# A gated recurrence with a highway layer on one core: units of eight blocks joined in pairs on freely named PSUM banks, and outputs stored by 1 MB transfers

## The chip, the cores and the metric

The kernel runs on one core of one Trainium2 chip. The metric is the device time of one execution in microseconds (us). A core has five engines with their own instruction streams: TensorE (PE, its weight loads shown apart as PEld), VectorE (DVE), ScalarE (ACT), GpSimd (POOL) and SyncE (SP, which here only issues transfers). PSUM is the accumulator memory, eight banks of 2 KB in each of 128 partitions; SBUF is the working memory.

## The reference

Four sequences of 6336 steps and 256 channels go through a gated recurrence, and each token of the result through a highway layer. Inputs and output are float32.

```python
def _attn_ref(x, f_logit, lower_bound):
    sig = 1.0 / (1.0 + np.exp(-f_logit))
    f = lower_bound[None, None, :] + (1.0 - lower_bound[None, None, :]) * sig
    i = 1.0 - f
    for t in range(S):
        h = f[:, t] * h + i[:, t] * x[:, t]
        y[:, t] = h
    return y

def _moe_ref(x, w_h, w_t, b_t):          # x is y as (25344, 256)
    H = np.maximum(x @ w_h, 0.0)
    T = 1.0 / (1.0 + np.exp(-(x @ w_t + b_t)))
    return T * H + (1.0 - T) * x
```

## The kernel before

With cc = 1 - lower_bound, the kernel takes u = sigmoid(-f_logit), so that i = cc u and f = 1 - cc u (ncc is -cc). The scan runs on y/cc, and cc is multiplied into the weights, into a diagonal matrix `diag` and into d.

The 25344 tokens are cut into 198 blocks of 128, and these into 28 units (`parts`, L42) of 2, 2, 4, then 23 times 8, then 4 and 2 blocks. A token of the stream lies in a partition with its neighbours: in a unit of eight blocks partition p holds eight tokens in a row, so that a load is 1 MB of 8 KB rows. Each unit passes through these steps, most of them once for each half h of the channels:

- l, x: one transfer each, issued on SP (L232 to L242).
- u: sigmoid on ACT, all of the unit at once (L247).
- b: products u x, in bf16 with two tokens packed side by side, on POOL, or on DVE where the token has a v (L250 to L257). Their tile is bv.
- i: PE transposes u into uT (PSUM, L259 to L263). f: 1 - cc uT, on ACT or DVE (L265 to L274).
- p: PE transposes the packed pairs of bv as float32 words into bT (PSUM, L276 to L283).
- s: the scan y = f y + bT on DVE, 1024 tokens in one instruction, chained to the unit before (L295 to L301).
- z, g: matmuls of y with the two weights (L303 to L320; L113 is the same matmul without a new load of weights). t: sigmoid of z, on ACT (L322 to L324). d: max(ncc y, g) on DVE (L326 to L329). e: d = d t, in two pieces, on POOL or DVE (L331 to L334).
- o: output matmuls that turn blocks back to token rows, with columns of y and d as weights and `diag` and an identity as data, four blocks in one two-bank PSUM tile op (L339 to L349). A block's columns lie `g` apart, and g is 4 in a unit of eight blocks.
- c: copy of op to an SBUF tile o of 4 KB a partition (L351 to L358). w: its store, 512 KB in 4 KB rows, issued on SP (L360 to L362).

The loops are written out as one string, `order`: each token is a step letter, a unit, a half or piece, and a buffer slot. All steps are pinned, so each engine runs its instructions in the order of the string, and SP issues loads and stores in that order too. Tokens k are idle matmuls that keep PE going. `shared` (L176) makes a POOL instruction follow a DVE one.

PSUM is split into two slots of one bank (a0, a1: uT and bT) and three of two banks (b0 to b2: z, g and op). SBUF has four o tiles of 4 KB. In the middle of the program l uses three buffers and x four.

Of the kernel before, what the change touches and what calls it, by code (L numbers as in the profile page):

```python
# [11 lines left out]
FP32 = mybir.dt.float32  # L12
# [7 lines left out]
def kernel(  # L20
# [10 lines left out]
    nc = tc.nc  # L31
# [10 lines left out]
    parts = [2] * 2 + [4] + [8] * 23 + [4] + [2]  # L42
    units, at = [], 0
    for nb in parts:
        units.append((nb, at, {2: (0, 1), 4: (0, 1, 2), 8: (0, 2, 4)}[nb], {2: (0, 256, 512), 4: (0, 512, 1024), 8: (0, 1024, 2048)}[nb]))
        at += nb * P
# [3 lines left out]
f0.0v:0 x5:5 f0.1v:1 WH p0.0:0 WT p0.1:1 k*4:0 s0.1:0 l6:5 x6:0 i2.0:1 b1.0:0 s0.0 f2.0:1 i1.0:0 z0.1:0 f1.0v:0 g0.1:1  # L50
g0.0:2 d0.1:0 b2.0:1 d0.0 p1.1:1 t0.1:0 i1.1:0 z0.0:0 k*4:1 b2.1 f1.1v:2 s1.1:1 p1.0:0 t0.0 p2.0:1 s1.0 e0.0 s2.0:2
z1.1:0 e0.1 u3:0 i2.1:0 z1.0:1 g1.1:2 b3.0:0 d1.1:1 p2.1:1 f2.1:0 g1.0:2 s2.1 t1.0:0 b3.1v d1.0 i3.0:0 k*4:1 t1.1
f3.0:1 g2.0:0 o0.0:1 i3.1:0 e1.1 e1.0 u4:1 d2.0:0 f3.1:0 p3.0:1 c0.0:0 s3.0:0 b4.1:1 z2.1:2 k*4:0 o1.0:0 b4.0 p3.1:0
s3.1 z2.0:1 w0.0 l7:0 t2.1:0 g2.1:2 c1.0:1 d2.1 i4.0:1 t2.0 k*4:0 e2.0 f4.0:1 e2.1 g3.0:0 w1.0 p4.0:0 u5:0 i4.1:1
z3.0:1 f4.1:0 b5.1:0 o2.0:2 p4.1:1 b5.0 t3.0:0 c2.0:2 w2.0 g3.1:1 x7:1 d3.0:1 s4.0:1 s4.1 u6:1 l8:1 i5.1:0 z3.1:0
p5.1:1 e3.0v f5.1:1 t3.1 z4.1:2 i5.0:0 b6.0:1 d3.1 f5.0:0 e3.1 g4.1:1 g4.0:0 t4.1:1 x8:2 u7:0 p5.0:0 s5.1:2 i6.0:1
d4.1:0 f6.0:1 o3.1*1:2 z4.0:1 s5.0 i7.0:1 d4.0 b6.1 c3.1:0 p6.0:0 s6.0:3 e4.1 z5.1:2 w3.1 b7.0:0 g5.1:0 l9:0 f7.0:0
d5.1:2 i6.1:1 t4.0 g5.0:1 i7.1:0 t5.1:0 f6.1:2 d5.0 o3.0:2 b7.1 p6.1:1 f7.1:1 x9:0 c3.0:1 e4.0v w3.0 e5.1 l10:2 u8:0
z5.0:0 p7.0:0 o4.1:1 s6.1 o4.0:2 c4.1:0 t5.0 i8.1:1 c4.0:2 s7.0:0 g6.0:1 u9:1 w4.1 f8.1:0 w4.0 g6.1:0 p7.1:0 l11:1
b8.1:1 x10:1 d6.0:0 b8.0 z6.0:2 s7.1 t6.0:1 z6.1:1 e5.0 i9.0:1 e6.0 p8.1:0 f9.0:1 o5.1:2 i8.0:1 d6.1 t6.1 f8.0:2  # L60
c5.1:0 g7.1:0 e6.1 w5.1 k*4:1 b9.0:0 p8.0:1 u10:0 s8.1:1 z7.0:1 t7.0:0 d7.1:1 i9.1:0 o6.1:0 s8.0 g7.0:2 c6.1v:1 l12:0
# [24 lines left out]
p22.1:1 t21.0:0 o19.1:2 l25:1 o19.0:1 d21.1:1 w18.0 w18.1 x24:0 p23.1:0 u25:0 s22.1 c19.0:0 b24.0:0 s23.1:2 g22.0:0
d22.0:2 i23.0:1 z22.0:1 x25:2 c19.1:1 z22.1:2 f23.0:0 p23.0:0 i25.0:1 t22.0:2 o20.0:0 g22.1:1 s23.0 w19.0 b24.1 t22.1
e22.0 g21.0:2 i24.0:0 c20.0:2 d22.1 g23.1:0 f25.0:1 w19.1 f24.0:0 i24.1:1 d21.0 d23.1:3 l26:0 e22.1v x26:1 f24.1:2
o20.1:1 g23.0:2 d23.0 p24.0:0 s24.0:1 b25.0:1 i25.1:1 c20.1:0 w20.0 l27:1 b25.1 z23.1:0 u26:1 f25.1:3 z21.1:1 p24.1:1
x27:3 o22.0:2 t23.1:1 b26.0:0 s24.1 e21.0v t21.1 c22.0:1 z23.0:0 p25.0:0 e21.1 o22.1:1 t23.0 z24.1:2 u27:0 i26.0:1  # L90
g24.0:0 s25.0:0 c22.1:2 f26.0:0 b26.1 z24.0:1 d24.0:0 p25.1:1 t24.1:2 i26.1:0 w20.1 e23.0 t24.0 o21.0:2 e23.1 g24.1:0
f26.1:1 c21.0:0 e24.0 o21.1:1 s25.1 p26.0:0 c21.1:3 p26.1:1 d24.1 s26.1:3 z25.1:2 w22.0 t25.1:0 g25.1:0 w22.1 w21.0
d25.1:1 o23.0:1 w21.1 s26.0 o23.1:2 i27.1:1 c23.0:1 z25.0:0 b27.0:0 w23.0 c23.1:0 g26.0:1 g25.0:2 t25.0 e24.1v d26.0:2
d25.0 i27.0:0 e25.1 e25.0v w23.1 f27.0:0 z26.1:0 o24.0:1 f27.1:1 p27.0:0 p27.1:1 z26.0:2 s27.0:2 s27.1 t26.1:1 c24.0:2
o25.0:0 t26.0 g26.1:1 w24.0 o24.1:2 d26.1 z27.0:1 c24.1v:0 c25.0:1 t27.0:0 o25.1:0 c25.1:3 e26.0 g27.0:1 d27.0:0 e26.1
o26.0:2 w25.0 w24.1 z27.1:1 t27.1 e27.0v c26.0:2 w25.1 w26.0 g27.1:0 d27.1 e27.1v o27.0:0 c27.0:1 w27.0
"""

    NU = len(units)
# [3 lines left out]
    st = [dict() for _ in range(NU)]  # L103
# [15 lines left out]
    extra = [0]  # L119

    def busy(t):
        for k in range(extra[0]):
            if k == 0:
                pin(nc.tensor.matmul(t[:, :512], zeros[:, :P], zeros, start=True, stop=True))
            else:
                pin(again(t[:, :512], zeros[:, :P], zeros, True, True))

    def one_bank(slot, dtype, name):
        t = ps.tile([P, NB * P], dtype, tag=f"a{slot}", name=name)
        busy(t.bitcast(FP32))  # L130
        return t

    def two_banks(slot, name):
        t = ps.tile([P, NB * P], FP32, tag=f"b{slot}", name=name)
        busy(t)
        return t
# [13 lines left out]
    for _ in range(8):  # L150
        nc.tensor.matmul(once["idle"][:, :512], zeros[:, :P], zeros, start=True, stop=True)
# [251 lines left out]
```

## Time and profile before

| | |
|---|---|
| median of 3 runs | 212.07 us (211.65 to 212.75) |
| span of the profiled execution, first to last instruction | 209.0 us |
| the profiled execution's own time | not recorded; the median is 3.1 us above its span |
| granted TensorE clock | 0.998 |
| busy: PE, DVE, ACT, POOL | 197.0, 194.8, 191.1, 176.2 us |
| DMA | 78.67 MB, 376 GB/s over the span |

Rows of the profile read so: a line of the kernel, an engine, an operation, the tiles written and read with partitions x elements, the count; behind the first bar the busy time in us and the mean ns of one; behind the second the idle time of the engine just before, and what ended it. A busy PE counts overlapped matmuls once. In a row of the time line the start and the duration come first. A row on a DMA has the issuing queue, the count, the KB of each and the median us from issue to landing.

### The profile page before, as it was taken

What the parts mean: (1) busy time and instruction counts of PE and PEld (TensorE: products, weight loads), DVE (VectorE), ACT (ScalarE), POOL (GpSimd) and SP (SyncE); (2) the same over time, 40 slices, a digit from 0 to 9 for tenths busy, and PEclk for the clock granted to TensorE, in tenths of its full rate; (3) what the DMA queues carried; (4) which work ended last, traced back from release to release, by engine and by line L of the source; (5) the groups of instructions that cost most, each with busy time, mean ns of one, the idle gap of its engine ahead of it and who ended that gap; (6) DMA issues with size and microseconds to landing.
All of it is one profiled execution on the core that took longest, in us unless ns stands there. A gap on an engine that the chain in (4) does not pass through costs nothing.

```text
span 209.0 us, 4656 instructions
## 1 busy us (share of the span) xinstructions
PE 197.0 (94%) x1852; PEld 135.3 (65%) x1852; DVE 194.8 (93%) x159; ACT 191.1 (91%) x185; POOL 176.2 (84%) x101
## 2 busy tenths in 40 slices
PE   7989998999899999899999999999999999999991
PEld 2446575686576577558676667575677776777680
DVE  0789999999999999999999999999999999999971
ACT  4368999999999999999999999999999999997972
POOL 3076998989997887997999899788999999989740
PEclk9999999999999999999999999999999999999999
DMA  6999999999999999999999999999999999655567
GB/s 174 367 419 423 416 417 421 416 423 372 422 408 351 387 427 413 416 417 412 410 420 416 423 418 424 408 425 412 426 421 400 379 405 341 267 204 201 199 278 279
DMA packets 15980, 78.67 MB, mean 376 GB/s; under 512 B 1748, under 2 KB 2264, under 8 KB 10072
## 3 DMA queue, kind: packets, MB, share of 16 engines
q1 hardware_dynamic: 15952, 78.39, 93.6%
q8 instruction: 14, 0.23, 0.5%
q14 instruction: 6, 0.05, 0.1%
q10 hardware_dynamic: 8, 0.00, 0.0%
HBM read 52.43 MB, written 25.95 MB: 375 GB/s over the span
## 4 chain that ended last, share of the span: by engine, by line
PE 50%; DVE 14%; ACT 12%; DMA 9%; issue 8%; POOL 4%; SPq 1%; DVEq 0%; ACTq 0%; POOLq 0%
DVE y L299 10%; PE op L347 7%; PE op L348 7%; PE z L311 7%; PE bT L282 6%; DMA x<-in_x_dram 6%; PE z L113 6%; PE g L311 6%; PE g L113 5%; PE uT L262 5%; ACT f L273 4%; DVE d L328 4%; ACT o L357 4%; POOL bv L255 3%; DMA l<-in_f_logit_dram 3%
## 5 line engine op out<-in xcount | busy, mean ns | idle before, releaser
L255 POOL TENSOR_TENSOR bv<-u,x 128x1024 bf16<-128x1024 f16 (+1 forms) x51 | 103.2, 2046 | 17.2 <-DVE y L299 9.3
L299 DVE TENSOR_TENSOR_SCAN y<-f,y,bT 128x1024 bf16<-128x1024 f16 (+5 forms) x54 | 106.8, 1991 | 1.0 <-PE bT L282 0.3
L334 POOL TENSOR_TENSOR d<-d,t 128x1024 bf16<-128x1024 bf16 (+2 forms) x39 | 73.0, 1888 | 7.8 <-DVE d L334 4.1
L328 DVE SCALAR_TENSOR_TENSOR d<-y,ncc,g 128x1024 bf16<-128x1024 bf16 (+2 forms) x56 | 62.9, 1140 | 1.6 <-PE g L311 1.0
L324 ACT ACTIVATE t<-z,bt 128x1024 bf16<-128x1024 f32 (+2 forms) x56 | 58.4, 1075 | 2.3 <-PE z L311 1.9
L273 ACT ACTIVATE f<-uT,ncc 128x1024 f16<-128x1024 f16 (+2 forms) x51 | 56.4, 1120 | 3.5 <-PE uT L262 3.2
L247 ACT ACTIVATE u<-l 128x2048 f16<-128x2048 f32 (+2 forms) x28 | 49.6, 1774 | 5.1 <-DMA l<-in_f_logit_dram 4.5
L357 ACT COPY o<-op 128x1024 f32<-128x1024 f32 (+1 forms) x48 | 48.9, 1047 | 2.3 <-PE op L348 1.7
L347 PE MATMUL op<-diag,y 128*128 128x128 f16 x396 | 49.4, 219 | 1.1 <-DVE d L328 0.6
L348 PE MATMUL op<-ident_b,d 128*128 128x128 bf16 x396 | 49.4, 219 | 0.1
L348 PEld LDWEIGHTS <-d 128*128 128x128 bf16 x396 | 44.0, 113 | 4.6 <-issue 1.6
L347 PEld LDWEIGHTS <-y 128*128 128x128 bf16 x396 | 44.2, 113 | 1.8
L311 PE MATMUL z<-y,w_sb 128*128 128x512 bf16 (+1 forms) x112 | 39.5, 367 | 0.5 <-ACT o L357 0.5
L311 PE MATMUL g<-y,w_sb 128*128 128x512 bf16 (+1 forms) x112 | 39.2, 367 | 0.1
L113 PE MATMUL z<-y,w_sb 128*128 128x512 bf16 x92 | 34.9, 379 | 0.0
L113 PE MATMUL g<-y,w_sb 128*128 128x512 bf16 x92 | 34.8, 379 | 0.0
L282 PE MATMUL bT<-ident_f,bv 128*128 128x128 f32 x198 | 31.4, 277 | 2.7 <-POOL bv L255 1.1
L262 PEld LDWEIGHTS <-u 128*128 128x128 f16 x396 | 26.3, 98 | 11.2 <-issue 4.8
L262 PE MATMUL uT<-ident_h,u 128*128 128x128 f16 x396 | 31.1, 220 | 2.2 <-ACT f L273 1.0
L311 PEld LDWEIGHTS <-w_sb 128*128 128x128 f16 x224 | 21.4, 98 | 15.5 <-DVE y L299 0.4
L282 PEld LDWEIGHTS bT<-ident_f,bv 128*128 128x128 f32 x198 | 22.6, 141 | 11.5 <-POOL bv L255 2.3
L113 PEld LDWEIGHTS <-w_sb 128*128 128x128 f16 x184 | 18.0, 98 | 16.2 <-issue 1.8
(36 smaller groups left out, 61.9 us busy)
## 6 DMA issues: line engine op xcount, KB each, us to landing
out_dram<-o SPq DMA_DIRECT2D x48, 512.0 KB, 7.0
l<-in_f_logit_dram SPq DMA_DIRECT2D x23, 1024.0 KB, 11.1
x<-in_x_dram SPq DMA_DIRECT2D x23, 1024.0 KB, 10.8
l<-in_f_logit_dram SPq DMA_DIRECT2D x2, 512.0 KB, 6.9
x<-in_x_dram SPq DMA_DIRECT2D x2, 512.0 KB, 7.0
l<-in_f_logit_dram SPq DMA_DIRECT2D x3, 256.0 KB, 3.2
x<-in_x_dram SPq DMA_DIRECT2D x3, 256.0 KB, 7.3
out_dram<-o SPq DMA_DIRECT2D x3, 256.0 KB, 6.7
```

What stands on the lines that cost most here:

```text
L113: return pe.add_instruction(mybir.InstMatmult(name=nc.get_next_instruction_name(), start_tensor_calc=start, stop_tensor_calc=stop, tile_si ...
L255: shared(pin(e.tensor_mul(st[n]["bv"][:, a:c].rearrange("p k d j -> p k j d"), st[n]["u"][:, 2 * a:2 * c].rearrange("p (k j) d -> p k j d" ...
L262: pin(nc.tensor.transpose(uT[:, j * P:(j + 1) * P], st[n]["u"][:, j, h * P:(h + 1) * P], ident_h))
L273: pin(nc.scalar.activation(to, of, AF.Identity, scale=ncc[:, h:h + 1], bias=1.0))
L282: pin(nc.tensor.transpose(words[:, k:k + g * (P - 1) + 1:g], pair, ident_f))
L299: pin(nc.vector.tensor_tensor_scan(y[:, c:e], st[n]["f", h][:, c:e], st[n]["bT", h][:, c:e], 0.0 if fresh else carry[h], op0=ALU.mult, op1 ...
L311: pin(nc.tensor.matmul(p[:, a:e], w, half(n, "y", ki)[:, a:e], start=ki == 0, stop=ki == NH - 1))
L324: pin(nc.scalar.activation(half(n, "t", m), st[n]["z", m][:, :tokens(n)], AF.Sigmoid, bias=bt[:, m:m + 1]))
L328: pin(nc.vector.scalar_tensor_tensor(half(n, "d", m), half(n, "y", m), ncc[:, m:m + 1], st[n]["g", m][:, :tokens(n)], op0=ALU.mult, op1=AL ...
L334: shared(pin(e.tensor_mul(st[n]["d"][:, a:c], st[n]["d"][:, a:c], st[n]["t"][:, a:c])), not eng)
L347: pin(nc.tensor.matmul(o, half(n, "y", h)[:, cols], diag[:, h], start=True, stop=False))
L348: pin(nc.tensor.matmul(o, half(n, "d", h)[:, cols], ident_b, start=False, stop=True))
```

## The change

There are 21 units now. Seven of them are pairs of eight-block parts: 16 blocks, 2048 tokens, of which f is one instruction of 2048 elements and s one scan of 2048 (cut only where a sequence ends). Loads, u and the transposes i and p stay at eight blocks. z, g, t, d and e go by chunks of eight blocks (`chunk`), so in a pair twice. New tokens B and E do both pieces of b or e in one instruction of 2048. PSUM is a single tile; every token names the banks that it uses. The output matmuls of an eight-block chunk take columns eight apart (`cl`) in place of four, the copies fill one o tile of 8 KB a partition, and one transfer stores the chunk: 1 MB of 8 KB rows. There are two such o tiles, and five buffers each of l and x.

```diff
-    parts = [2] * 2 + [4] + [8] * 23 + [4] + [2]
+    parts = [(2,), (2,), (4,), (8,), (8,), (8,), (8,), (8, 8), (8, 8), (8, 8), (8, 8), (8, 8), (8, 8), (8, 8), (8,), (8,), (8,), (8,), (8,), (4,), (2,)]
...
     order = """
-l0:0 l1:1 x0:0 l2:2 wh wt x2:1 x1:2 u0:0 l3:3 pc:0 u2:1 x3:3 cc u1:2 l4:0 i0.1:0 x4:4 dg b0.0v:0 i0.0:1 k*16:1 l5:4
+pc:0 k*4:1 l0.0:0 u0.0:0 i0.0.1:1 i0.0.0:2 l1.0:1 u1.0:1 i1.0.0:3 i1.0.1:4 x1.0:0 cc b1.0.0:0 p1.0.1:0 p1.0.0:5 dg
...
+    psum = ps.tile([P, BANKS * BANK], FP32, tag="psum", name="psum")
+
+    class Banks:
+        def __init__(self, named, dtype=FP32):
+            at = [int(c) for c in named]
...
+    def chunk(n, q):
+
+        nb = sum(units[n][1])
+        return q * NB, min(NB, nb - q * NB)
...
+    def do_B(eng, slot, n, s):
+        products(eng, slot, n, s, 0, 2)
...
+        f = sb([P, 2 * NB * P], FP16, "f", slot)
...
+        y = sb([P, 2 * NB * P], BF16, "y", slot)
...
+    def do_E(eng, slot, n, q):
+        gated(eng, n, q, 0, 2)
...
-            cols = slice(j0 * P + j, j0 * P + j + g * (P - 1) + 1, g)
...
+            whole = slice(c0 * P + j, c0 * P + j + cl * (P - 1) + 1, cl)
+            cols = slice(j, j + cl * (P - 1) + 1, cl)
             for h in range(NH):
...
-        o = sb([P, 4, D], FP32, "o", slot)
...
+            st[n]["o", q] = sb([P, NB * D], FP32, "o", slot)
...
+    def do_w(eng, slot, n, q, r):
+        c0, cl = chunk(n, q)
+        o = st[n]["o", q].rearrange("p (j d) -> p j d", d=D)
+        pin(nc.sync.dma_start(rows(out, units[n][0], c0, c0 + cl), o[:, :cl]))
```

Numbers behind the names below are of the tiles. On DVE, this is the place where blocks 56 to 71 are scanned, before:

```order
L328 SCALAR_TENSOR_TENSOR d_955<-y_856,ncc_94,g_957 128x1024
L299 SCALAR_TENSOR_TENSOR y_997<-f_939,y_856,bT_975 128x1024
L299 SCALAR_TENSOR_TENSOR y_997<-f_801,y_856,bT_1006 128x1024
L299 SCALAR_TENSOR_TENSOR y_1043<-f_941,y_997,bT_1033 128x1024
L334 TENSOR_TENSOR d_866<-d_866,t_864 128x1024
L328 SCALAR_TENSOR_TENSOR d_1092<-y_997,ncc_94,g_1059 128x1024
L328 SCALAR_TENSOR_TENSOR d_1092<-y_997,ncc_94,g_1082 128x1024
L299 SCALAR_TENSOR_TENSOR y_1043<-f_1057,y_997,bT_1087 128x1024
```

Units 9 and 10 (y_997, y_1043) take four scans. After, on DVE, the same blocks are unit 8, whose two halves are y_869 and y_914:

```order
L317 SCALAR_TENSOR_TENSOR y_869<-f_767,y_805,psum_61 128x2048
L360 SCALAR_TENSOR_TENSOR d_908<-y_805,ncc_92,psum_61 128x1024
L317 SCALAR_TENSOR_TENSOR y_914<-f_749,y_838,psum_61 128x2048
L360 SCALAR_TENSOR_TENSOR d_908<-y_838,ncc_92,psum_61 128x1024
L360 SCALAR_TENSOR_TENSOR d_953<-y_805,ncc_92,psum_61 128x1024
L360 SCALAR_TENSOR_TENSOR d_959<-y_914,ncc_92,psum_61 128x1024
L360 SCALAR_TENSOR_TENSOR d_981<-y_869,ncc_92,psum_61 128x1024
```

Two scans of twice the length stand for the four, with one d between them; `p8.0.1:01` and `p8.1.1` put the second scan's bT into banks 0 and 1, which the first scan reads.

On DVE, the end of the program before:

```order
L328 SCALAR_TENSOR_TENSOR d_2905<-y_2825,ncc_94,g_2970 128x512
L355 COPY o_2995<-op_2974 128x1024
L328 SCALAR_TENSOR_TENSOR d_3024<-y_2945,ncc_94,g_3021 128x256
L334 TENSOR_TENSOR d_3024<-d_3024,t_2999 128x256
L328 SCALAR_TENSOR_TENSOR d_3024<-y_2945,ncc_94,g_3055 128x256
```

Behind these rows the second piece of d_3024 is multiplied by t in the same way. The end on DVE after:

```order
L317 SCALAR_TENSOR_TENSOR y_2641<-f_2530,y_2583,psum_61 128x256
L360 SCALAR_TENSOR_TENSOR d_2636<-y_2583,ncc_92,psum_61 128x512
L374 TENSOR_TENSOR d_2636<-d_2636,t_2607 128x512
L360 SCALAR_TENSOR_TENSOR d_2655<-y_2641,ncc_92,psum_61 128x256
L360 SCALAR_TENSOR_TENSOR d_2655<-y_2638,ncc_92,psum_61 128x256
L403 COPY o_2687<-psum_61 128x512
```

The last gate product has moved from DVE to POOL, whose last instruction is now `d_2655<-d_2655,t_2649 128x512`, and the last copy from ACT to DVE.

On ACT, the place after at which the two o tiles come closest: o_1524 is the second chunk of unit 9, and o_1634, the first chunk of unit 10, takes the same slot 0.

```order
L405 COPY o_1524<-psum_61 128x1024
L259 ACTIVATE u_1571<-l_1459 128x2048
L259 ACTIVATE u_1591<-l_1526 128x2048
L353 ACTIVATE t_1607<-psum_61,bt_93 128x1024
L405 COPY o_1634<-psum_61 128x1024
L298 ACTIVATE f_1646<-psum_61,ncc_92 128x2048
```

Before, four o tiles of half the size took turns, each with a store of its own.

Around these, the startup has another order (l0, l1, x1, x0, the two weights, l2, x2, l3, x3; `order` of before has l0, l1, x0, l2, the weights, x2, x1, l3, x3), and there are 55 idle matmuls in place of 57.

More of the change, by code (lines that the diff above doesn't have):

```diff
@@ L148 @@
     nc.vector.memset(zeros, 0.0)
-    once["idle"] = two_banks(2, "idle")
-    for _ in range(8):
-        nc.tensor.matmul(once["idle"][:, :512], zeros[:, :P], zeros, start=True, stop=True)
+    for _ in range(6):
+        pin(nc.tensor.matmul(psum[:, 7 * BANK:], zeros[:, :P], zeros, start=True, stop=True))
     prm = sb([2 * NH, P], FP32, "prm")
@@ L190, in do_pc @@
     def do_pc(slot):
-        once["prmT"] = ps.tile([P, 2 * NH], FP32, tag=f"b{slot}", name="prmT")
+        once["prmT"] = Banks(slot).one(0)[:, :2 * NH]
         pin(nc.tensor.transpose(once["prmT"], prm, ident_f[:2 * NH, :2 * NH]))
@@ L223, in do_WH, with do_k @@
                                                op0=ALU.mult, op1=ALU.add))
-            last = pin(nc.vector.tensor_scalar(w_sb[:, 0, h, rest], w_raw[:, 0, h, rest], cc[:, h:h + 1], None,
+            pin(nc.vector.tensor_scalar(w_sb[:, 0, h, rest], w_raw[:, 0, h, rest], cc[:, h:h + 1], None,
                                                op0=ALU.mult))
-        shared(last, False)
-    def rows(full, n, j0, j1):
-        at = units[n][1]
+    def do_k(slot, times):
+        out = Banks(slot).one(0)
+        for k in range(times):
+            if k == 0:
+                pin(nc.tensor.matmul(out, zeros[:, :P], zeros, start=True, stop=True))
+            else:
+                pin(again(out, zeros[:, :P], zeros, True, True))
@@ new lines, in load, with do_l, do_x, do_u @@
+        pin(nc.sync.dma_start(t[:, :subs[s]], rows(src, at, j0, j0 + subs[s])))
+        st[n][name, s] = t
+    def do_l(eng, slot, n, s):
+        load(n, s, "l", logits, slot)
+    def do_x(eng, slot, n, s):
+        load(n, s, "x", xs, slot)
+    def do_u(eng, slot, n, s):
+        nb = units[n][1][s]
+        u = sb([P, NB, D], FP16, "u", slot)
+        pin(nc.scalar.activation(u[:, :nb], st[n]["l", s][:, :nb], AF.Sigmoid, scale=-1.0))
+        st[n]["u", s] = u
+    def do_b(eng, slot, n, s, k):
+        products(eng, slot, n, s, k, k + 1)
@@ L306, in ffn @@
         for ki in range(NH):
             w = w_sb[:, k, ki, m * P:(m + 1) * P]
-            for a in range(0, N, 512):
-                e = min(a + 512, N)
+            for a in range(0, cl * P, BANK):
+                e = min(a + BANK, cl * P)
+                data = st[n]["y", ki][:, c0 * P + a:c0 * P + e]
                 if a == 0:
-                    pin(nc.tensor.matmul(p[:, a:e], w, half(n, "y", ki)[:, a:e], start=ki == 0, stop=ki == NH - 1))
+                    pin(nc.tensor.matmul(p.part(a, e), w, data, start=ki == 0, stop=ki == NH - 1))
@@ new lines, in half, with do_t, do_d @@
+    def half(n, q, name, h):
+        M = chunk(n, q)[1] * P
+        return st[n][name, q][:, h * M:(h + 1) * M]
+    def do_t(eng, slot, n, q, m):
+        flat(n, q, "t", slot)
+        z = st[n]["z", q, m].all(chunk(n, q)[1] * P)
+        pin(nc.scalar.activation(half(n, q, "t", m), z, AF.Sigmoid, bias=bt[:, m:m + 1]))
+    def do_d(eng, slot, n, q, m):
+        flat(n, q, "d", slot)
+        c0, cl = chunk(n, q)
+        g = st[n]["g", q, m].all(cl * P)
+        y = st[n]["y", m][:, c0 * P:(c0 + cl) * P]
+        pin(nc.vector.scalar_tensor_tensor(half(n, q, "d", m), y, ncc[:, m:m + 1], g,
+                                           op0=ALU.mult, op1=ALU.max))
@@ new lines, in do_o @@
+    def do_o(eng, slot, n, q, r):
+        op = Banks(slot)
+        j0, j1 = blocks(n, q, r)
+        c0 = chunk(n, q)[0]
+        cl = chunk(n, q)[1]
+        for j in range(j0 - c0, j1 - c0):
+            whole = slice(c0 * P + j, c0 * P + j + cl * (P - 1) + 1, cl)
+            cols = slice(j, j + cl * (P - 1) + 1, cl)
+            for h in range(NH):
+                at = (j + c0 - j0) * D + h * P
+                o = op.part(at, at + P)
+                pin(nc.tensor.matmul(o, st[n]["y", h][:, whole], diag[:, h], start=True, stop=False))
+                pin(nc.tensor.matmul(o, half(n, q, "d", h)[:, cols], ident_b, start=False, stop=True))
+        st[n]["op", q, r] = op
@@ L358, in do_c @@
-        st[n]["o", q] = o
-    def do_w(n, q, eng, slot):
-        j0, j1 = blocks(n, q)
-        pin(nc.sync.dma_start(rows(out, n, j0, j1), st[n]["o", q][:, :j1 - j0]))
+            pin(nc.scalar.copy(to, op))
+    def do_w(eng, slot, n, q, r):
+        c0, cl = chunk(n, q)
+        o = st[n]["o", q].rearrange("p (j d) -> p j d", d=D)
+        pin(nc.sync.dma_start(rows(out, units[n][0], c0, c0 + cl), o[:, :cl]))
     here = locals()
```

309 lines of the change are left out of this document (146 added, 163 removed).

## The prediction

> **What bounds the kernel now.** I read the engine shares first, then the chain by engine, then the busy time of each engine by stage (columns: stretch, its length, then busy time of PE, PEld, DVE, ACT and POOL, clock, DMA share, GB/s).
>
> ```profile
> span 209.0 us, 4656 instructions
> PE 197.0 (94%) x1852; PEld 135.3 (65%) x1852; DVE 194.8 (93%) x159; ACT 191.1 (91%) x185; POOL 176.2 (84%) x101
> PE 50%; DVE 14%; ACT 12%; DMA 9%; issue 8%; POOL 4%; SPq 1%; DVEq 0%; ACTq 0%; POOLq 0%
> 30.00:200.00 170.00, 165.49 (x1612) 116.03 (x1610) 168.68 (x118) 166.66 (x157) 156.36 (x77) 1.00 0.95 382
> 30.00:160.00 130.00, 125.51 (x1218) 87.72 (x1216) 129.28 (x89) 129.06 (x117) 120.21 (x58) 1.00 1.01 412
> 160.00:200.00 40.00, 39.98 (x398) 28.30 (x396) 39.39 (x30) 37.60 (x41) 36.16 (x20) 1.00 0.74 285
> ```
>
> The chain gives PE half of the path, but a chain follows one of several equal routes here. Between 30 and 200 us DVE is idle for 170.00 - 168.68 = 1.3 us, ACT for 3.3, PE for 4.5, POOL for 13.6. Up to 160 us the DMA engines are full too (1.01). From 160 us PE has nothing idle. So in the middle an edit can gain little unless it takes work off DVE, and it loses as soon as a new wait falls on DVE or PE. DVE's other idle time, 209.0 - 194.8 - 1.3 = 12.9 us, lies in the start and the tail.
>
> The sum is made against this execution's span, 209.0 us. The median of the runs is 212.07, so 3.1 us lie outside the span, and I take them as unchanged.
>
> **DVE's work.** Its instructions and their prices (busy, mean ns of one, idle before):
>
> ```profile
> L299 DVE TENSOR_TENSOR_SCAN y<-f,y,bT 128x1024 bf16<-128x1024 f16 x40 | 92.9, 2336 | 0.5
> L299 DVE TENSOR_TENSOR_SCAN y<-f,y,bT 128x512 bf16<-128x512 f16 x4 | 5.1, 1276 | 0.5 <-PE bT L282 0.3 <-ACT t L324 0.2
> 27.61 4.58 DVE L299 TENSOR_TENSOR_SCAN y<-f,y,bT 128x1024 bf16<-128x1024 f16 x2
> L271 DVE TENSOR_SCALAR f<-uT,ncc 128x256 f16<-128x256 f16 x4 | 1.8, 480 | 0.4 <-PE uT L262 0.4
> L271 DVE TENSOR_SCALAR f<-uT,ncc 128x1024 f16<-128x1024 f16 x1 | 1.3, 1278 | 0.0
> L255 DVE TENSOR_TENSOR bv<-u,x 128x1024 bf16<-128x1024 f16 x1 | 1.3, 1337 | 0.0
> L255 DVE TENSOR_TENSOR bv<-u,x 128x512 bf16<-128x512 f16 x1 | 0.7, 725 | 0.0
> L334 DVE TENSOR_TENSOR d<-d,t 128x1024 bf16<-128x1024 bf16 x15 | 10.7, 724 | 0.2
> L334 DVE TENSOR_TENSOR d<-d,t 128x256 bf16<-128x256 bf16 x2 | 0.6, 292 | 0.2
> L355 DVE COPY o<-op 128x1024 f32<-128x1024 f32 x3 | 3.6, 1204 | 0.1
> ```
>
> A scan costs (2336 - 1276)/512 = 2.07 ns an element, which leaves 2336 - 1024 x 2.07 = 216 ns fixed. Two scans in a row take 4.58 us, so the second begins 2.24 us after the first, and 0.09 of the fixed part lies under its neighbour. The change makes 48 scans of 62, with the same elements: 14 x (0.216 - 0.09), or 1.8 us less.
>
> The order gives part of that back by what it puts on DVE. Forget gates f: three of 1024 and one of 256 in place of one and four, 3 x 1.278 + 0.48 - (1.278 + 4 x 0.48) = +1.1. Products bv: one of 2048 (by the slope of the two rows 2.56) for 1.34 + 0.73, +0.5. Gate products d: five of 1024 fewer (-3.6), two of 2048 more (by the slope 1.30 each) and two of 512 more (0.44 each), -0.1. Copies: one of 1024 fewer (-1.2), two of 512 more (0.7 each by half and a fixed part), +0.2. Sum: -1.8 + 1.1 + 0.5 - 0.1 + 0.2 = **-0.1 us**. The bound engine gets no less to do.
>
> **ACT and POOL.**
>
> ```profile
> L273 ACT ACTIVATE f<-uT,ncc 128x1024 f16<-128x1024 f16 x45 | 52.7, 1185 | 1.3 <-PE uT L262 1.1
> L273 ACT ACTIVATE f<-uT,ncc 128x512 f16<-128x512 f16 x4 | 2.9, 713 | 1.9 <-PE uT L262 1.8
> L255 POOL TENSOR_TENSOR bv<-u,x 128x1024 bf16<-128x1024 f16 x45 | 96.3, 2162 | 7.9 <-DVE d L334 4.4 <-DMA x<-in_x_dram 1.4 <-PE uT L262 1.1
> L255 POOL TENSOR_TENSOR bv<-u,x 128x512 bf16<-128x512 f16 x6 | 7.0, 1174 | 9.3 <-DVE y L299 9.3
> ```
>
> ACT's f has (1185 - 713)/512 = 0.92 ns an element and 241 ns fixed; 28 of 1024 become 14 of 2048, at most 14 x 0.24 = 3.4 us. POOL's products have 186 ns fixed and ten are merged, 1.9 us. Neither engine is the tightest (3.3 and 13.6 us idle), so I count both at **0**. That DVE is the cover says what would be late next: nothing on ACT can pull in a DVE that has 1.3 us idle. The DMA engines move the same bytes in longer rows: 0.
>
> **The start.**
>
> ```profile
> 10.28 1.26 DVE L299 TENSOR_TENSOR_SCAN y<-f,bT 128x256 bf16<-128x256 f16 x2
> 16.54 2.15 POOL L255 TENSOR_TENSOR bv<-u,x 128x1024 bf16<-128x1024 f16 x1 [0.30 <-DMA x<-in_x_dram]
> ```
>
> The new order loads both first x units before the weights, so the first scan can go some 1.7 us before 10.28 by the bytes ahead of it. But unit 3's inputs have the same bytes ahead as before, and its products, which waited for x until 16.54 on POOL in two pieces, now take 2.56 us in one piece on DVE. I expect the scans of unit 4 where they were (27.61). **0**, between -1 and +1.
>
> **The tail.**
>
> ```profile
> L334 POOL TENSOR_TENSOR d<-d,t 128x512 bf16<-128x512 bf16 x4 | 4.6, 1164 | 1.8 <-ACT t L324 1.6 <-DVE d L328 0.2
> 204.16 0.29 DVE L334 TENSOR_TENSOR d<-d,t 128x256 bf16<-128x256 bf16 x1
> 205.04 0.59 ACT L357 COPY o<-op 128x512 f32<-128x512 f32 x1 [0.31 <-ACT o L357]
> ```
>
> The last gate product was a 0.29 us piece on DVE, the other half being done already. Now both halves are one instruction on POOL, 1.16 us, behind the last d, and before the last output matmuls: +0.9. The last copy goes to DVE (0.7 for 0.59): +0.1. **+1.0**, between +0.5 (POOL's start hides half) and +1.3.
>
> **The waits of pairs.** A pair's bT fills two banks and is read by one scan of about 4.5 us, so PE gets those banks back later. The tightest place in the order is unit 8: its second bT is transposed into the very two banks which the first scan has just left, and DVE has one d (1024) for that time.
>
> ```profile
> L328 DVE SCALAR_TENSOR_TENSOR d<-y,ncc,g 128x1024 bf16<-128x1024 bf16 x46 | 57.3, 1262 | 0.6 <-issue 0.3 <-PE g L113 0.2
> 189.93 0.44 PE bT L282 x4
> DVE y L299 <- PE bT L282: 0.3, 1, 0.3
> ```
>
> Eight transposes at 0.44/4 = 0.11 us and about 0.3 of latency are 1.2 us, against 1.26 of d: just covered. It is the tightest place that I found. From below: DVE's 1.3 us of idle time all vanish, -1.3. From above: all 14 pair scans bare, 14 x 1.2 = +16.8. I take a doubling of the idle time in the part of the program that is paired (seven pairs are 112 of 198 blocks, 57%): 0.57 x 1.3 = **+0.7**, since the nearest row, DVE's wait for bT, is 0.3 us in all now.
>
> **The stores.** 1 MB stores run through two slots of 8 KB in place of four of 4 KB, the same bytes in SBUF, but a slot is free only when all 1 MB has landed.
>
> ```profile
> out_dram<-o SPq DMA_DIRECT2D x48, 512.0 KB, 7.0
> l<-in_f_logit_dram SPq DMA_DIRECT2D x23, 1024.0 KB, 11.1
> L324 ACT ACTIVATE t<-z,bt 128x1024 bf16<-128x1024 f32 x46 | 52.9, 1186 | 0.4 <-PE z L113 0.4
> L247 ACT ACTIVATE u<-l 128x2048 f16<-128x2048 f32 x23 | 45.7, 1986 | 0.6 <-POOL d L334 0.6
> SPq L362 <- ACT o L357: 130.2, 42, 8.5
> ```
>
> A 512 KB store lands 7.0 us after its issue; 512 KB more at 412 GB/s makes 8.3, and the 1 MB load's 11.1 is the upper bound. Before, no copy waited for a store. SP already spends 130.2 us waiting at stores for copies, and now loads queue behind a store until both halves are copied; five buffers each of l and x are the cover. I count it at 0, and keep its price for a rival.
>
> **The weights of the output matmuls.** Each output matmul has 128 columns of y or d as weights. They lay 8 bytes apart in an 8-block unit (step of four), 4 bytes apart in a 2-block unit; now they lie 16 bytes apart.
>
> ```profile
> L348 PEld LDWEIGHTS <-d 128*128 128x128 bf16 x4 | 0.4, 98 | 0.1
> L348 PEld LDWEIGHTS <-d 128*128 128x128 bf16 x99 | 11.1, 114 | 0.8 <-DVE d L334 0.3
> 165.04 0.22 PE L348 MATMUL op<-ident_b,d 128*128 128x128 bf16 x1
> 165.10 0.22 PE L347 MATMUL op<-diag,y 128*128 128x128 f16 x1
> ```
>
> The first row is from a 2-block unit (18.8 to 19.6 us), the second from 160 to 200 us. Doubling the step cost 16 ns of a weight load, and yet the matmuls follow each other every 0.06 us, so loads overlap and the 16 ns are hidden. I count another 16 ns at 0; below nothing is excluded, since no column gets nearer to the next. [...]
>
> **Sum.** 209.0 - 0.1 + 0 + 1.0 + 0.7 = 210.6 us of span; with 3.1 outside, **213.7 us**, 0.8% slower. About 0.5%, 1.1 us, is what a measurement of this kernel can tell from no change.
>
> **Rivals.**
> - *No change that can be measured* (211.0 to 213.1): the waits stay at 1.3 us and POOL starts the last gate product early, so the sum is 209.0 - 0.1 + 0.5 + 3.1 = 212.5. For it: the zero sum on DVE.
> - *Faster, 210.2*: the free banks take all of DVE's 1.3 us of idle time, the earlier first scan gives 1.0, half the tail is hidden: 209.0 - 0.1 - 1.3 - 1.0 + 0.5 + 3.1. Against it: DVE's work hardly falls, so there is no more to win than idle time.
> - *Weight loads set PE's pace, 221.0*: 23 x 8 x 4 = 736 loads of 16 bytes' step, each 16 ns longer with nothing hidden, are 11.8 us; PE's 4.5 idle take some, and 7.3 go on top of 213.7. It decides once a load exceeds what overlap hides. If the pace fell to the 0.11 of the fp32 transposes, 736 x 0.05 = 37 less 4.5 would make 246. Against it: 0.06 us held at both steps.
> - *Copies wait for the two store slots, 218.9*: between the copy that fills slot 0 for unit 9's second chunk and the next that needs slot 0, ACT has two u and a t, 2 x 1.99 + 1.19 = 5.2 us, where a landing takes 8.3: 3.1 short. Three more rooms, counted the same way, are 5.7, 6.5 and 7.3: 2.6 + 1.8 + 1.0. Of 8.5 in all, ACT's idle 3.3 take some: +5.2. It decides where a landing takes over 5.2 us.
>
> **Chances.** Forecast (212.1 plus more than 1.1, up to about 215.2) 0.38, no change 0.25, faster 0.19, weight loads 0.10, store slots 0.08. Faster 0.19, same 0.25, slower 0.38 + 0.10 + 0.08 = 0.56. The range: 210.0 takes in the faster case's own figure, and half its chance (0.10) lies below; 221.0 takes in both slow rivals at their figures, and about half of the weight loads' chance (0.05) lies above, so 0.15 is left out. The forecast's own range is 213.1 to 215.2.
>
> **What would show it.** Right: DVE idle between 30 and 200 us near 2 us, its busy time within 0.5 us of 194.8, the last gate product on POOL at about 1.16 us, output matmuls still every 0.06 us, no ACT wait for a store. Wrong: output matmuls further apart (weight loads); ACT copies that wait for a DMA (store slots); DVE idle under 0.5 us in the middle or the scans of unit 4 well before 27.6 (faster); a stretch in which PE and DVE take turns to wait for bT (the pairs' waits at more than I took).

## The result

The changed kernel takes 218.32 us (median of 6 runs, 218.06 to 218.79); the kernel before takes 212.33 us (6 runs). The ratio is 1.029, with a 95% interval of 1.026 to 1.033. The profiled execution has a span of 216.5 us; 1.8 us of the median lie outside it.

The page and the stages of the changed kernel (stretch, its length, busy time of PE, PEld, DVE, ACT and POOL, clock, DMA share, GB/s):

```profile
span 216.5 us, 4545 instructions
PE 199.2 (92%) x1850; PEld 140.5 (65%) x1850; DVE 197.4 (91%) x143; ACT 188.7 (87%) x171; POOL 172.4 (80%) x82
30.00:120.00 90.00, 84.06 (x810) 60.14 (x808) 89.29 (x51) 87.25 (x69) 84.98 (x32) 1.00 1.01 412
120.00:150.00 30.00, 26.21 (x243) 18.34 (x242) 25.47 (x15) 25.07 (x22) 26.06 (x12) 0.94 0.93 348
150.00:180.00 30.00, 30.00 (x305) 22.41 (x304) 29.02 (x20) 27.89 (x27) 22.64 (x11) 1.00 0.97 387
30.00:200.00 170.00, 160.20 (x1545) 115.42 (x1543) 163.51 (x96) 158.51 (x135) 152.79 (x61) 0.99 0.95 375
```

The medians differ by 6.0 us and the two profiled spans by 7.5: in every execution with both on record 1.7 to 1.9 us lie outside the span, so the execution profiled before was about 1.3 us faster than its median (3.1 - 1.8). Of the 7.5 us that the span grew, 2.6 are DVE's busy time (197.4 for 194.8) and 4.9 its idle time. The idle time lies in one place: between 120 and 150 us DVE waits 30.00 - 25.47 = 4.5 us, where the rest of the middle waits 2.0. There the DMA engines move 348 GB/s instead of 412, and the granted clock is 0.94.

The transfers that SP issues around that place, with ACT's waits for stores, in the changed kernel (start, duration):

```profile
109.86 0.44 SPq L247 DMA_DIRECT2D x<-in_x_dram  x1
125.68 0.34 SPq L410 DMA_DIRECT2D out_dram<-o  x1
126.12 0.40 SPq L247 DMA_DIRECT2D x<-in_x_dram  x1
126.57 0.90 SPq L410 DMA_DIRECT2D out_dram<-o  x1
ACT o L405 <- DMA out_dram<-o: 3.7, 3, 2.8
130.81 1.01 ACT L405 COPY o<-psum 128x1024 f32<-128x1024 f32 x1 [0.53 <-DMA out_dram<-o]
138.42 1.01 ACT L405 COPY o<-psum 128x1024 f32<-128x1024 f32 x1 [2.82 <-DMA out_dram<-o]
```

For 15 us SP issues nothing: it stands at the store of unit 9's second chunk until that chunk's second copy. The store of the first chunk, whose copies were done by 122 us, stands behind it. Then both go within a microsecond, with a load between them. The first to go, the second chunk's, lands 5.0 us after its issue, at 130.7, when unit 10's first chunk has waited 0.53 us for that slot. The other lands 11.8 us after its issue, behind that store and the load, and unit 10's second chunk waits 2.8 us for its slot. What follows is in the chain, in order of time, in the stage behind, and in PE's waits (the last row):

```profile
126.57 11.78 DMA out_dram<-o
138.42 1.02 ACT o L405
139.48 1.13 PE psum L283 x16
140.61 0.43 PE psum L330
140.00:144.00 4.00, 4.00 (x20) 1.71 (x17) 2.56 (x2) 4.00 (x4) 3.48 (x2) 0.57 0.84 346
PE psum L283 <- ACT o L405: 2.7, 1, 2.7
```

PE waited 2.7 us while ACT held its banks, and came back at a granted clock of 0.57 on the mean of these 4 us: a matmul of 512 columns takes 0.43 us of the chain, 0.22 elsewhere. DVE's 4.5 us of waiting are longer than ACT's 0.5 + 2.8 for stores; the slow stretch of PE fits that, and the run with three slots below bears it out.

### The profile page after: what moved, and what is told of

It is laid out like the page before. It is cut to its first block, busy times and chain, and to the rows that moved or that the text cites. A ratio compares the mean times of both kernels' runs of the same rounds, so it can differ in the third digit from the quotient of the medians.

```text
span 216.5 us, 4545 instructions
## 1 busy us (share of the span) xinstructions
PE 199.2 (92%) x1850; PEld 140.5 (65%) x1850; DVE 197.4 (91%) x143; ACT 188.7 (87%) x171; POOL 172.4 (80%) x82
## 4 chain that ended last, share of the span: by engine, by line
PE 55%; ACT 14%; DVE 11%; DMA 11%; issue 4%; POOL 2%; SPq 0%; DVEq 0%; ACTq 0%; POOLq 0%
PE psum L330 15%; PE psum L142 14%; DMA out_dram<-o 11%; PE psum L392 7%; PE psum L391 7%; DVE y L317 6%; PE psum L308 6%; PE psum L283 5%; ACT u L259 4%; ACT o L405 4%; ACT t L353 3%; ACT f L298 3%; POOL bv L274 2%; PE psum L161 1%; DVE d L360 1%
## 5 line engine op out<-in xcount | busy, mean ns | idle before, releaser
L274 POOL TENSOR_TENSOR bv<-u,x 128x1024 bf16<-128x1024 f16 (+2 forms) x39 | 100.4, 2591 | 23.3 <-DMA x<-in_x_dram 10.8
L317 DVE TENSOR_TENSOR_SCAN y<-f,y,psum 128x1024 bf16<-128x1024 f16 (+6 forms) x40 | 103.7, 2614 | 1.7 <-PE psum L308 0.7
L374 POOL TENSOR_TENSOR d<-d,t 128x1024 bf16<-128x1024 bf16 (+3 forms) x32 | 71.8, 2254 | 15.8 <-DVE d L360 8.7
L330 PE MATMUL psum<-y,w_sb 128*128 128x512 bf16 (+1 forms) x224 | 78.4, 372 | 4.4 <-DVE y L317 2.0
L142 PE MATMUL psum<-y,w_sb 128*128 128x512 bf16 x184 | 70.7, 384 | 0.0
L360 DVE SCALAR_TENSOR_TENSOR d<-y,ncc,psum 128x1024 bf16<-128x1024 bf16 (+2 forms) x56 | 62.4, 1145 | 3.4 <-PE psum L142 2.2
L353 ACT ACTIVATE t<-psum,bt 128x1024 bf16<-128x1024 f32 (+2 forms) x56 | 55.7, 1022 | 5.9 <-PE psum L142 4.6
L298 ACT ACTIVATE f<-psum,ncc 128x1024 f16<-128x1024 f16 (+3 forms) x38 | 48.8, 1310 | 6.7 <-PE psum L283 6.7
L391 PE MATMUL psum<-diag,y 128*128 128x128 f16 x396 | 52.4, 224 | 2.0 <-ACT f L298 1.5
L392 PE MATMUL psum<-ident_b,d 128*128 128x128 bf16 x396 | 52.6, 225 | 1.3 <-POOL d L374 1.1
L374 DVE TENSOR_TENSOR d<-d,t 128x1024 bf16<-128x1024 bf16 (+3 forms) x16 | 11.1, 711 | 0.2 <-ACT t L353 0.2
```

The lines of the kernel that those rows point to most:

```text
L142: return pe.add_instruction(mybir.InstMatmult(name=nc.get_next_instruction_name(), start_tensor_calc=start, stop_tensor_calc=stop, tile_si ...
L274: shared(pin(e.tensor_mul(st[n]["bv", s][:, a:c].rearrange("p k d j -> p k j d"), st[n]["u", s][:, 2 * a:2 * c].rearrange("p (k j) d -> p ...
L317: pin(nc.vector.tensor_tensor_scan(y[:, c:e], st[n]["f", h][:, c:e], data, 0.0 if fresh else carry[h], op0=ALU.mult, op1=ALU.add))
L330: pin(nc.tensor.matmul(p.part(a, e), w, data, start=ki == 0, stop=ki == NH - 1))
L353: pin(nc.scalar.activation(half(n, q, "t", m), z, AF.Sigmoid, bias=bt[:, m:m + 1]))
L360: pin(nc.vector.scalar_tensor_tensor(half(n, q, "d", m), y, ncc[:, m:m + 1], g, op0=ALU.mult, op1=ALU.max))
```

## The experiments

Theory A is that the store part (1 MB transfers through two slots) makes the loss; theory B is that the weight loads with a step of 16 bytes do; theory C is that the pairs, the start and the tail do. Ratios are to the kernel before on the same chip, with 95% intervals.

**Three slots.** Edit: `c` tokens take slots 0, 1, 2 in turn, and `w_raw` uses the third slot's space at the start.

```diff
+    w_raw = pool.tile([P, 2, NH, D], FP32, tag="o2", name="w_raw")
```

> The changed kernel with three o tiles of 8 KB instead of two (the weights' raw copy of the start lies in the third one's space). Theory A, two store slots: ACT's waits for stores (3.7 us in the trace after) vanish, PE no longer falls to half speed between 140.6 and 144 us, and DVE's 4.5 us of idle time between 130 and 150 us go, so 218.3 - 4.5 = 213.8 us. Theory B, the weight loads with 16 bytes' step: they stay, and PE is the bound, so no less than 217.3 us.

Measured: 1.026 (1.020 to 1.032). The first wait went, the other stayed. ACT's waits for stores in this kernel, PE's for ACT, and the stage:

```profile
ACT o L405 <- DMA out_dram<-o: 3.4, 1, 3.4
PE psum L283 <- ACT o L405: 2.8, 1, 2.8
120.00:150.00 30.00, 25.96 (x263) 19.55 (x265) 26.95 (x16) 26.62 (x24) 26.15 (x12) 1.00 0.92 349
```

With slots taken in turn, unit 10's first chunk has a free one, but its second chunk again takes the slot of unit 9's first, whose store still stands behind the second chunk's on SP. In this profile PE waited 2.8 us, as long as in the changed kernel, and kept its clock, and DVE waited 30.00 - 26.95 = 3.05 us there instead of 4.5. The time hardly changed: not theory A's number, and after this run B still stood.

**Step four, 1 MB transfers.**

```diff
-            whole = slice(c0 * P + j, c0 * P + j + cl * (P - 1) + 1, cl)
+            whole = slice(c0 * P + b0 + jj, c0 * P + b0 + jj + g * (P - 1) + 1, g)
...
+        to = out[at:at + cl * P, :].rearrange("(r p j) d -> p r j d", p=P, j=g)
```

> The changed kernel with output columns four apart again (8 bytes), two o tiles and one 1 MB transfer a chunk, now of 4 KB rows. Theory B, weight loads: output matmuls return from 0.061 to 0.055 us apart, 736 x 0.006 = 4.4 us less PE work, and 214 us. Theory A, store slots: the waits at 130 to 140 us stay, within 1 us of 218.3.

Measured: 1.032 (1.027 to 1.036), no gain. The output matmuls did return to their old pace (0.056 us apart from 160 to 200 us), but ACT's waits for stores took 5.1 us, where the changed kernel has 3.7:

```profile
ACT o L407 <- DMA out_dram<-o: 5.1, 4, 2.5
```

The stores' rows are 4 KB here instead of 8 KB, so this run differs from the changed kernel in more than the weights.

**Store part undone.** Step four, and each half of a chunk in its own 4 KB tile, stored by its own 512 KB transfer; both transfers stand where the one stood.

```diff
+        for r in st[n]["done", q]:
+            j0, j1 = blocks(n, q, r)
+            o = st[n]["o", q, r].rearrange("p (j d) -> p j d", d=D)
+            pin(nc.sync.dma_start(rows(out, units[n][0], j0, j1), o[:, :j1 - j0]))
```

> The changed kernel with its store part undone: columns four apart, each half of a chunk in an o tile of its own (four of 4 KB) and stored by a 512 KB transfer of 4 KB rows, both issued at the place of the one. If stores and weights are the whole loss: 212.3, as before the change. Theory A alone: a slot comes free when its own half has landed, 213.8 to 216. Theory B alone: 214. A third theory, C, that the pairs and the start cost by themselves: over 214.

Measured: 1.0125 (1.008 to 1.017). So 1.7 points of the 2.9 went, in the same SBUF; ACT still waits 2.7 us for stores:

```profile
ACT o L408 <- DMA out_dram<-o: 2.7, 2, 1.8
```

The tiles and stores are of the old size and number again, so what is left of the loss comes with the rest of the change. Both halves of a chunk are stored together, behind the second copy; a store right behind each copy was not tried.

**Half stores, step eight.** The same with the columns eight apart, so only the weight loads differ.

```diff
+            pin(nc.sync.dma_start(whole[:, j0 - c0:j1 - c0], o[:, :j1 - j0]))
```

> As the run with the store part undone (1.0125 of before), but with the columns eight apart, so that only the weight loads differ from it: four o tiles of 4 KB and 512 KB transfers of 4 KB rows. Theory A, store slots: within 0.4% of 1.0125. Theory B, weight loads: 736 x 0.006 = 4.4 us of PE work come back and lie on the path from 150 us on, up to 1.033.

Measured: 1.014 (1.010 to 1.019), with about the waits of the run before:

```profile
ACT o L406 <- DMA out_dram<-o: 2.4, 2, 2.2
```

Between these two runs the step makes 0.2 points, which intervals of 0.45 points each way can't tell from nothing. Theory B falls as the cause of the loss. Against the changed kernel the step is the same and only the store part differs: 1.029 to 1.014, so 1.5 points are the joined stores'.

**The weights' dependence.** `shared(last, False)` put back in do_dg, do_WT and do_WH.

> The changed kernel with the dependence restored that makes the next POOL instruction wait for DVE's preparation of diag and of the two weights. If the 2.17 us that one 128x128 weight product took on DVE (0.28 before) was the lock between the two engines, it is 0.28 again and the scans of unit 4 begin up to 1.9 us before 28.35. If the middle is bound by DVE the time falls by 1 to 1.9 us (216.4 to 217.3); if a later wait takes it, under 0.5 us (over 217.8).

Measured: 1.031 (1.027 to 1.035). The long instruction went, the time didn't. The group and its long instruction, with the POOL product beside it, in the changed kernel, then the group in this one:

```profile
L229 DVE TENSOR_SCALAR w_sb<-w_raw,cc 128x128 f16<-128x128 f32 x2 | 2.4, 1224 | 0.0
11.56 2.17 DVE L229 TENSOR_SCALAR w_sb<-w_raw,cc 128x128 f16<-128x128 f32 x1
11.47 2.17 POOL L274 TENSOR_TENSOR bv<-u,x 128x1024 bf16<-128x1024 f16 x1 [4.02 <-DMA x<-in_x_dram]
```

```profile
L231 DVE TENSOR_SCALAR w_sb<-w_raw,cc 128x128 f16<-128x128 f32 x2 | 0.5, 274 | 0.0
```

Scans of unit 4 begin at 28.55 us instead of 28.35: POOL's product now waits for DVE and starts at 12.72 us instead of 11.47, so the 1.9 us of DVE work were not on the path. Of the lock that the expectation supposes, the traces show this: DVE's instruction ended at 13.73 us, 0.09 after POOL's product beside it, and took 0.27 us where the two did not run side by side.

**The first chunk's store earlier.**

```diff
-l14.0:1 c9.0.1 o9.1.0:67 x13.1:4
+l14.0:1 c9.0.1 w9.0.0 o9.1.0:67 x13.1:4
```

> The changed kernel with one token moved: the store of unit 9's first chunk stands right behind its second copy, ahead of the store of the second chunk, which holds SP until 125.7 us. Theory A in a narrower form: not the number of slots but SP's order is the cause; the store is issued near 122 instead of 126.6 us, lands before 130, the copy of unit 10 that waited 2.8 us doesn't wait, PE keeps its clock, DVE loses 4.4 us of idle time between 130 and 150 us: 218.3 - 4.4 = 213.9 us, ratio 1.009. Theory B: 1.029 as before.

Measured: 1.022 (1.016 to 1.029). My narrower theory, SP's order alone, gives 1.009 and falls: the load x13.1, which went at 109.86, now stands behind the moved store until 123.29. The copy that had waited 2.8 us doesn't wait any more, but the one before it does: unit 10's first chunk, which had waited 0.53 us, waits 2.53 for the store of unit 9's second chunk, issued at 126.56 behind x13.1 and landed 7.0 us later (ACT's time line of this kernel):

```profile
133.68 1.01 ACT L405 COPY o<-psum 128x1024 f32<-128x1024 f32 x1 [2.53 <-DMA out_dram<-o]
```

**The same with step four, and with half stores.** The same token moved in two of the kernels above: the one with step four and 1 MB transfers, and the one with its store part undone.

> The same token moved, and the columns four apart with one 1 MB transfer of 4 KB rows. Against the run with the token alone it tells what 16 bytes' step costs once the stall is gone: theory B up to 4.4 us less PE work, 1.5 to 4.4 us off (PE has nothing idle from 150 us on), theory A under 0.5 us.

> The store part undone (1.0125) with the same token moved. It still had a copy that waited 1.8 us for a store at 138 us, and 1.5 us of DVE idle time between 120 and 150 us: both go, 214.2 - 1.5 = 212.7 us, ratio 1.005. If it stays at 1.0125, what is left comes from the pairs, the start and the tail.

Measured: 1.026 (1.021 to 1.031) and 1.010 (1.005 to 1.015). The first, against 1.022 for the moved token alone, is against theory B again. The second can't decide: 1.0125 lies within its interval, and 1.005 at its edge.

**Loads first.** In the changed kernel x13.0 and l15.0 go ahead of unit 9's stores, and the first chunk's store ahead of the second's.

```diff
-l14.0:1 c9.0.1 o9.1.0:67 x13.1:4
+l14.0:1 c9.0.1 o9.1.0:67 x13.1:4 x13.0:0 l15.0:2 w9.0.0
```

> The changed kernel with 1 MB stores and two slots as it is, but three tokens moved: the loads x13.0 and l15.0, whose buffers are free by then, go ahead of the two stores of unit 9, and the store of its first chunk (data ready first) ahead of that of the second. Theory A in the form that SP's order is the cause (a 1 MB store waits on SP 15.3 us for its second copy, loads that could go stand behind it, the DMA engines run dry near 125 us): 120 to 150 us carry over 390 GB/s instead of 348 and DVE loses 3 to 4.5 us of idle time there, ratio 1.010 to 1.016. Theory A in the form that the two slots are the cause, however SP is ordered: copies wait for a store as long as in the changed kernel (3.7 us), ratio 1.025 to 1.03.

Measured: 1.048 (1.043 to 1.054), worse than either form said. This kernel's stages and ACT's wait:

```profile
110.00:125.00 15.00, 13.89 (x140) 10.22 (x140) 15.00 (x10) 15.00 (x13) 13.17 (x6) 1.00 1.02 424
120.00:150.00 30.00, 20.85 (x175) 14.84 (x177) 19.56 (x13) 20.28 (x18) 19.29 (x10) 0.83 0.65 271
138.51 1.01 ACT L405 COPY o<-psum 128x1024 f32<-128x1024 f32 x1 [8.23 <-DMA out_dram<-o]
```

The DMA engines were kept full before the stores (424 GB/s), and for that the stores landed later: the store of unit 9's second chunk, issued at 125.68 as before, held its slot until 138.4, and the copy that had waited 0.53 us waited 8.2. Neither order comes near the kernel before. In the changed kernel SP holds back the loads, the DMA engines have little to do before that store (188 GB/s from 124 to 126 us), and it lands in 5 us; here it queues behind the loads and takes 12.7. Two slots of 1 MB have no room for that.

**The kernel before with 1 MB stores alone.** Step eight, two tiles of 8 KB, one transfer a unit where the later half's stood.

```diff
+        if st[n]["ws"] == (nb + 3) // 4:
+            pin(nc.sync.dma_start(rows(out, n, 0, nb), st[n]["o"][:, :nb]))
```

> The kernel before with the store part of the change alone: columns eight apart, two o tiles of 8 KB, one 1 MB transfer of 8 KB rows a unit, issued where the later half's store stood; no pairs. If the store part costs in itself what it costs in the changed kernel (1.5%, the difference between 1.029 and the run with half stores at 1.014): 212 + 3.2 = 215 us, more where two units' halves alternate. If it only costs with the pairs' order: within 0.5% of before.

Measured: 1.086 (1.080 to 1.092). ACT's waits for stores in it:

```profile
ACT o L361 <- DMA out_dram<-o: 15.4, 6, 6.9
```

The store part costs without any pair, and far more in an order that was laid out for four small tiles: 8.6%, some 18 us.

**Mended.** Half stores with step four, the loads first, the weights' dependence back.

> The changed kernel with all that the runs so far speak for: store part undone (1.0125), the loads ahead of unit 9's stores, and the DVE-POOL dependence of the weights restored. If what is left over before (2.7 us) came from waits of loads and stores at 120 to 150 us, 1.5 us more go, ratio 1.005; if from the pairs, the start and DVE's work (195.6 against 194.8 us), it stays at 1.010 to 1.013.

Measured: 1.027 (1.021 to 1.033), against my expectation. The dependence alone had changed nothing that could be measured, so what undoes the halves' gain is the new order of loads and stores; a copy of unit 10 now waits 5.75 us (ACT's time line of this kernel).

```profile
136.26 1.01 ACT L411 COPY o<-psum 128x1024 f32<-128x1024 f32 x1 [5.75 <-DMA out_dram<-o]
```

**Six half slots.** The kernel with the store part undone, with six tiles of 4 KB in turn instead of four (24 KB, as the three slots of 8 KB).

```diff
+        st[n]["o", q, r] = sb([P, 4 * D], FP32, "o", turn[0] % 6)
+        turn[0] += 1
```

> The changed kernel with the store part undone (1.0125) and six o tiles of 4 KB instead of four, each half of a chunk taking the next one; order as changed, the weights' raw copy of the start lies in the sixth. If the copies' waits for stores (2.7 us, with 1.5 us of DVE idle time at 120 to 150 us) are the rest of what room in SBUF can buy, they go and the time is 214.2 - 1.5 = 212.7 us, ratio 1.005. What then is left over 1.00 belongs to the pairs, the start and the tail. If the waits only move on, as in the run with three slots of 8 KB, the ratio stays at 1.012.

Measured: 211.56 us (12 runs, 210.72 to 212.48), 0.997 (0.995 to 0.9995). ACT's waits for stores, the stages and the busy times of this kernel:

```profile
ACT o L409 <- DMA out_dram<-o: 0.9, 1, 0.9
30.00:200.00 170.00, 161.70 (x1602) 114.88 (x1600) 168.33 (x101) 163.39 (x140) 157.32 (x64) 1.00 0.95 382
120.00:150.00 30.00, 28.08 (x283) 20.14 (x281) 29.35 (x17) 28.73 (x26) 27.93 (x13) 1.00 0.96 375
PE 193.2 (92%) x1850; PEld 134.6 (64%) x1850; DVE 196.5 (93%) x143; ACT 188.1 (89%) x171; POOL 172.0 (82%) x82
```

With the same pairs, nearly the same start and the same tail, the loss of 2.9% is gone and 0.3% is gained, just clear of no change. So theory A holds in this form: the o tiles come free too late. The step to half tiles (1.0125) and the step to six of them (0.997) each take about half. Three slots of 8 KB, with the same room, took off 0.3 points; there the tile is free only when both halves have been copied and landed. Theory C falls as a cost by itself; what the new order does is to need more room than the four tiles with which no copy waited before. Not tried: six half slots with the columns eight apart, and six in the kernel before. This kernel's profiled span is 210.7, 1.7 above that of before, with a median 0.8 below: the execution profiled here took 212.48 us, the highest of the 12, and that of before lay 1.3 below its median.

## Why the prediction was right or wrong

The direction and the range held; the likeliest time, 213.7, was 4.6 us short. The direction held by luck: with the stores' waits taken away (six half slots) the ratio is 0.997, so the pairs and the tail, which were to make the kernel slower, don't. The measured case was the rival with the store slots, priced at 218.9 and given 0.08. Its mechanism is the one that the runs show; that its time fits within 0.6 us is partly luck too, since it holds a tail of 1.0 us that did not come and 8.5 us of ACT's waits, of which 3.7 came.

- **The stores, counted at 0: this step failed.** Its landing time of 8.3 us was a median (7.0) plus 512 KB at 412 GB/s, the rate in the middle before. The trace after has 5.0 where the DMA engines had little to move (188 GB/s from 124 to 126 us) and 11.8 behind a store and a load, near the 11.1 of 1 MB loads that I had named as the upper bound. The rival's place was one copy early: unit 10's first chunk waited 0.53 us; its second waited 2.8, since both chunks' stores left SP together, the one that was ready first behind the other. Together with PE's slow stretch that is the measured price of the term: DVE's idle time from 30 to 200 us is 170.00 - 163.51 = 6.5 us, and 1.7 with six half slots, so +4.8 in place of 0. The landing time alone doesn't decide it. All stores of the changed kernel:

```profile
DMA to landing us min/median/max: 2.0/5.5/18.6
```

The 18.6 us are of a store issued at 65.07 us, and no copy waited for it: the next copy into that slot came late enough.

- **Waits of pairs, +0.7:** right. DVE's idle time from 30 to 200 us rose from 1.3 to 6.5, but with six half slots it is 170.00 - 168.33 = 1.7, so +0.4. At unit 8, which I took as the tightest, the d covers the transposes as reckoned: it runs from 69.05 to 70.31 us, the eight transposes from 69.19 to 70.28, and the second scan begins at 70.32. The 0.3 us of latency in that reckoning is the duration of one transpose, 0.27 us in the trace before. DVE waits 90.00 - 89.29 = 0.7 us in all from 30 to 120 us.
- **DVE's work, -0.1:** it was +2.6. A scan of 2048 went as reckoned (4468 ns, below; 4456 by the slope). 1.8 us of the 2.6 are the products of the weights in the start (2.4 us in two instructions, row L229 above, 0.6 before), which lost their dependence: with it restored DVE is busy for 195.6 us. That removal stood in the diff and I did not price it; restoring it gained no time. The other 0.8 us are not accounted for.

The scans of pairs and the start of unit 4's scans in the changed kernel:

```profile
L317 DVE TENSOR_TENSOR_SCAN y<-f,y,psum 128x2048 bf16<-128x2048 f16 x8 | 35.5, 4468 | 0.2 <-issue 0.2
28.35 4.57 DVE L317 TENSOR_TENSOR_SCAN y<-f,y,psum 128x1024 bf16<-128x1024 f16 x2
```

- **The start, 0:** +0.7 (28.35 for 27.61), within the stated bounds.
- **The tail, +1.0:** this step failed too; the parts came as priced, the sum did not. The gate product is on POOL at 1.15 us and the copy takes 0.69, but the last two d run together. From the first of them to the end it is 216.5 - 209.94 = 6.6 us, and 209.0 - 202.26 = 6.7 before.

The first of the last two d before, then the tail of the changed kernel:

```profile
202.26 0.48 DVE L328 SCALAR_TENSOR_TENSOR d<-y,ncc,g 128x256 bf16<-128x256 bf16 x1 [0.27 <-PE g L311]
209.94 0.86 DVE L360 SCALAR_TENSOR_TENSOR d<-y,ncc,psum 128x256 bf16<-128x256 bf16 x2
210.97 1.15 POOL L374 TENSOR_TENSOR d<-d,t 128x512 bf16<-128x512 bf16 x1 [6.54 <-DVE d L360]
212.98 0.69 DVE L403 COPY o<-psum 128x512 f32<-128x512 f32 x1 [2.18 <-PE psum L392]
```

- **The weight loads, counted at 0:** right in time, wrong in pace. A load grew by 32 ns, not 16, and matmuls are 0.061 us apart instead of 0.055 (changed kernel, 160 to 200 us; then two starts of many):

```profile
L392 PEld LDWEIGHTS <-d 128*128 128x128 bf16 x104 | 13.0, 146 | 0.6
160.47 0.23 PE L392 MATMUL psum<-ident_b,d 128*128 128x128 bf16 x1
160.53 0.23 PE L391 MATMUL psum<-diag,y 128*128 128x128 f16 x1
```

That is 736 x 0.006 = 4.4 us of PE work. From 160 to 200 us a load took 146 ns with columns 16 bytes apart (changed kernel, three slots, the kernel before with 1 MB stores) and 114 with 8 bytes (the kernel before, step four with 1 MB transfers, six half slots); no run shows why. The two runs that differ in the step alone lie 0.2 points apart, within their intervals. The 16 ns that the prediction adds to a load were half of what came. Whether the pace would cost time in a kernel without store waits was not tried.
- **What lies outside the span, 3.1 us:** 1.8 lie outside, in all runs that have both figures; the other 1.3 were the distance of the profiled execution before from its median. The sum starts from the median all the same, so this cost the forecast nothing.

## What to carry to other kernels

An output buffer came free here when its store had landed, not when it was issued (issued at 126.57 us, landed at 138.35, the waiting copy began at 138.42), and with transfers queued ahead that took 11.8 us where an emptied queue (188 GB/s from 124 to 126 us) gave 5.0. Joining two stores into one keeps the bytes and the buffer space, and yet doubles what must be filled, landed and freed at once. Count a slot from its first copy to the landing, with what the issuing queue holds before the store and the transfers ahead of it, and set that against the time of the next copy that needs the slot. Where the room was short, many small tiles did better than few large ones of the same bytes (1.014 for 1.029 in 16 KB; 0.997 for 1.026 in 24 KB, where the columns' step differs too).

## What was not expected of the hardware

- The clock granted to PE was 0.57 of full speed on the mean of 140 to 144 us, after PE had waited 2.7 us. In the run with three slots PE waited 2.8 us at the same place and kept 1.00, so the length of the wait alone doesn't decide it, and what does is open. DVE's idle time there was 4.5 us with the slow stretch and 3.05 without it, for the same waits of ACT for stores (3.4 us in both).
- One 128x128 instruction on DVE took 2.17 us instead of 0.28, to just after the end of a POOL product that ran beside it (13.73 and 13.64 us); with a dependence between the two it was back at 0.27.
- Two 1 MB stores issued 0.9 us apart landed after 5.0 and 11.8 us, the second behind the first and a load; over the execution a store's landing took up to 18.6 us.
